# Attention and two MLPs on one core: batch 0's q and k loaded to 128 partitions, empty products on TensorE, and a new order

## The chip, the core and the metric

The kernel runs on one core of a Trainium2 chip. The metric is the device time of one execution in microseconds (us); the kernel before was timed three times, and once more under the profiler. The engines are named as in the profile: PE is TensorE (PEld its weight loads), DVE is VectorE, ACT is ScalarE, POOL is GpSimd, and SP (SPq in a timeline) is SyncE, on whose queue all loads and stores of this kernel are issued.

## What is computed

```python
def _attn_ref(q, k, v):                      # q, k, v: 2 batches, 8 heads, 576 positions, 64 wide
    q_d = q.reshape(B, H, Sd, factor, D).mean(axis=3)     # factor 4, Sd = 144; k_d, v_d alike
    out_up = np.repeat(sm_attn(q_d, k_d, v_d), factor, axis=2)
    mask = np.abs(pos[:, None] - pos[None, :]) < factor
    scores = np.where(mask, scale * np.matmul(q, k.transpose(0, 1, 3, 2)), -1000000000.0)
    ...
    return out_up + np.matmul(softmax(scores), v)

def _moe_ref(x, w_in, w_out):                # x: 1152 x 512, w_in: 512 x 2048
    h = x @ w_in
    return np.where(h > 0.0, h, np.exp(np.minimum(h, 0.0)) - 1.0) @ w_out

def _moe2_ref(x, domain_probs, w1, w2):      # 4 experts, 512 x 1024 and 1024 x 512
    p = domain_probs / (domain_probs.sum(-1, keepdims=True) + 1e-09)
    for e in range(E):
        out += p[:, e:e + 1] * (np.maximum(x @ w1[e], 0.0) @ w2[e])
    return out
```

The attention's output, as 1152 rows of 512, is x of the first MLP, and that one's output is x of the second.

## The kernel before

The program is one stream of steps up to the second MLP. The steps stand in a string, ORDER, in the order in which they are issued; each engine does its share of them in that order. A step's name is a letter or two and numbers; 0 or 1 ahead of it is the batch. Behind a colon stands the engine that does it (v, a or g for VectorE, ScalarE, GpSimd) or, for a step that takes a PSUM bank, a number of empty products.

The steps of attention: LK loads q or k (ti is 0 for q, 1 for k). For batch 0 a load brings half the heads to 72 partitions, eight positions of each head in a row, and is issued as one DMA for 64 partitions and one for 8. CP copies a head pair so that it can be transposed, Tp transposes it on TensorE (four products of 72 columns), Te evicts the result to qkT. Batch 1's loads need no copy. PQ pools q or k over four positions; LV loads v for pooling, PVa and PVb pool it; VB loads a block of v for the local attention. GSp, GSm, GSx, GEr, GEm, GTp, GTe, GPp and GPe are the pooled attention (scores, maximum, exponential, sum, division, transposes, product with v); LSp to LPp are the local attention for a block of 64 queries, and LPa, LPh and LPl add both and write x as two parts, high and low. The steps of the first MLP: wF loads a quarter of a set of weights (1 MB), wA to wE round it, wH and wL split it; hp multiplies x by w_in for 128 hidden columns and 288 rows (12 products), ha, he, hd, hh and hl make the activation, yp multiplies it by w_out, ya evicts and adds up. mF, mS, mH, mL and nF, nH, nL prepare the second MLP's first weights. At C the attention's buffers are given back and the weights that follow load into them.

SyncE issues the loads in the order of the steps, each when its buffer is free. PSUM has eight banks, handed out in the order of the steps: a step on TensorE that takes the ninth waits until the first has been evicted. Ahead of everything, step W issues ten products of nothing. A step with a number behind its colon starts with that many products of 256 columns on the bank that it takes:

```python
        def bank(name, spare=0, uses=1):
            ...
            for _ in range(spare):
                nc.tensor.matmul(ps[:, :256], identb, junk.to_broadcast([P, 256]), start=True, stop=True)
```

In the kernel before no step has such a number.

## Time and profile before

| what | value |
|---|---|
| median of 3 timed runs | 689.39 us (688.63 to 689.83) |
| the profiled execution, its own time | 687.1 us |
| its span, first to last instruction | 685.3 us |
| mean granted TensorE clock | 0.974 |
| TensorE busy | 660.8 us (96%) |
| VectorE, ScalarE, GpSimd busy | 453.8, 303.4, 260.3 us |

The span is 1.8 us shorter than the execution's own time, which also holds what lies around the instructions. A granted clock of 1.00 is TensorE's upper level, 2.4 GHz, and 0.50 its lower, 1.2 GHz; a value between is a mean over a stretch. Products are pipelined, so a busy TensorE in these rows is one that has products under way.

### The profile page before, as it was taken

To read this page: it belongs to the slowest core of one execution; us is meant where nothing else is said; L and a number is where in the kernel's file an instruction comes from. 1 tells how busy PE (TensorE), PEld (TensorE's weight loads), DVE (VectorE), ACT (ScalarE), POOL (GpSimd) and SP (SyncE) were. 2 spreads that over 40 slices of the span, in tenths; PEclk is the share of its full clock that TensorE was granted. 3 is DMA by queue.
4 is the path that set the end of the run, shared out by engine and by line. 5 is a ranking of instruction groups with operands and counts; after the bars stand their busy time and mean duration, and the time that the engine had idled before them with its cause. 6 is when DMAs were issued, how large, how long until landed. Compare 5 with 4: busy or idle time off the path is not lost.

```text
span 685.3 us, 12161 instructions
## 1 busy us (share of the span) xinstructions
PE 660.8 (96%) x4804; PEld 607.2 (89%) x4804; DVE 453.8 (66%) x887; ACT 303.4 (44%) x801; POOL 260.3 (38%) x231
## 2 busy tenths in 40 slices
PE   6698998999999999999999999999999999999997
PEld 4477998899999999998889899898898998998986
DVE  3689998844767868489847567476385475663752
ACT  3489977655656545644413223134043132241310
POOL 1422334533521231547735434445175254344000
PEclk7579999999999999999999999999999999999999
DMA  8987336303024130010110211011101101110012
GB/s 169 213 228 176 117 77 83 82 1 125 12 113 121 65 124 1 1 62 2 61 62 1 62 62 49 14 62 62 61 2 62 62 1 61 63 62 1 1 46 93
DMA packets 40943, 46.69 MB, mean 68 GB/s; under 512 B 23094, under 2 KB 23094, under 8 KB 40886
## 3 DMA queue, kind: packets, MB, share of 16 engines
q1 hardware_dynamic: 40886, 45.91, 24.1%
q8 instruction: 38, 0.62, 0.4%
q14 instruction: 19, 0.16, 0.1%
HBM read 43.55 MB, written 2.36 MB: 67 GB/s over the span
## 4 chain that ended last, share of the span: by engine, by line
PE 83%; DVE 5%; DMA 4%; ACT 3%; SPq 2%; POOL 1%; issue 1%; DVEq 0%; ACTq 0%; POOLq 0%
PE psH L263 37%; PE psZ L263 29%; PE psY L263 13%; DMA raw<-in_v_dram 3%; SPq L513 2%; PE psX L677 1%; PE psS L616 1%; DMA vb<-in_v_dram 1%; PE psP L660 1%; DMA raw<-in_q_dram 1%; SPq L500 1%; PE psO L790 1%; ACT le L635 1%; PE psGT L768 1%; PE psT L567 1%
## 5 line engine op out<-in xcount | busy, mean ns | idle before, releaser
L263 PE MATMUL psZ<-wr,h 128*128 128x512 f32 x864 | 199.2, 390 | 0.0
L263 PEld LDWEIGHTS psZ<-wr,h 128*128 128x128 f32 x864 | 161.3, 188 | 33.1
L999 DVE TENSOR_TENSOR u<-psH,u 128x288 f32<-128x288 f32 x224 | 97.9, 454 | 30.6 <-PE psH L263 23.5
L263 PE MATMUL psH<-x,w 128*128 128x288 f32 x768 | 111.5, 299 | 0.2
L1060 DVE SCALAR_TENSOR_TENSOR oacc<-psZ,pn,oacc 128x512 f32<-128x512 f32 x63 | 47.2, 750 | 96.3 <-PE psZ L263 96.3
L263 PE MATMUL psY<-g,w 128*128 128x288 f32 x768 | 109.1, 296 | 1.2 <-DVE acc L885 1.2
L263 PEld LDWEIGHTS psH<-x,w 128*128 128x128 f32 x768 | 105.4, 190 | 1.1 <-issue 0.5
L263 PEld LDWEIGHTS psY<-g,w 128*128 128x128 f32 x768 | 103.9, 188 | 2.1 <-DVE acc L885 1.5
L1002 ACT ACTIVATE h<-u 128x288 fp32r<-128x288 f32 x128 | 56.6, 443 | 97.9 <-DVE u L999 95.7
L1006 DVE SCALAR_TENSOR_TENSOR h<-u,h 128x288 fp32r<-128x288 f32 x128 | 88.2, 693 | 7.0 <-ACT h L1002 5.2
L263 PE MATMUL psH<-xt,ws 128*128 128x288 f32 x576 | 82.3, 295 | 1.2 <-POOL xt L921 1.0
L263 PEld LDWEIGHTS psH<-xt,ws 128*128 128x128 f32 x576 | 78.5, 188 | 1.7 <-POOL xt L921 1.3
L1016 ACT ACTIVATE u<-psH 128x288 f32<-128x288 f32 x32 | 12.9, 403 | 141.1 <-PE psH L263 141.1
L857 POOL TENSOR_TENSOR g<-gf,g 128x288 fp32r<-128x288 f32 x40 | 35.1, 888 | 81.4 <-ACT g L852 81.1
L263 PE MATMUL psH<-xbo,wa 128*128 128x288 f32 x384 | 61.5, 295 | 0.0
L369 POOL TENSOR_TENSOR st<-raw 128x256 f32<-128x256 f32 x32 | 27.1, 846 | 77.8 <-DMA raw<-in_moe_w_dram 77.2
L263 PEld LDWEIGHTS psH<-xbo,wa 128*128 128x128 f32 x384 | 55.4, 188 | 1.2
L397 POOL TENSOR_TENSOR ws<-st,ws 128x1024 fp32r<-128x1024 f32 x16 | 38.9, 2431 | 44.9 <-ACT ws L391 44.9
L397 POOL TENSOR_TENSOR wa<-raw,wa 128x256 fp32r<-128x256 f32 (+1 forms) x32 | 34.9, 1094 | 41.4 <-ACT wa L391 41.4
L435 POOL TENSOR_TENSOR wr<-raw,wr 128x1024 fp32r<-128x1024 f32 x16 | 39.4, 2479 | 17.3 <-ACT wr L430 17.3
L845 DVE SCALAR_TENSOR_TENSOR gf<-m,psH 128x288 f32<-128x288 f32 x64 | 28.6, 450 | 22.3 <-ACT m L840 15.5
L852 ACT ACTIVATE g<-gf 128x288 fp32r<-128x288 f32 x64 | 26.4, 439 | 25.6 <-DVE gf L845 19.5
(99 smaller groups left out, 819.4 us busy)
## 6 DMA issues: line engine op xcount, KB each, us to landing
raw<-in_moe_w_dram SPq DMA_DIRECT2D x16, 1024.0 KB, 5.3
raw<-in_moe_w_in_dram SPq DMA_DIRECT2D x8, 1024.0 KB, 6.4
raw<-in_moe_w_out_dram SPq DMA_DIRECT2D x8, 1024.0 KB, 6.6
vb<-in_v_dram SPq DMA_DIRECT2D x16, 160.0 KB, 5.7
out_dram<-oacc SPq DMA_DIRECT2D x9, 256.0 KB, 2.0
raw<-in_v_dram SPq DMA_DIRECT2D x4, 512.0 KB, 11.9
raw<-in_q_dram SPq DMA_DIRECT2D x2, 512.0 KB, 9.6
raw<-in_k_dram SPq DMA_DIRECT2D x2, 512.0 KB, 7.4
```

The lines of the kernel that those rows point to most:

```text
L263: nc.tensor.matmul(ps, wt[a], xt[b], start=first and n == 0, stop=last and n == 2)
L369: nc.gpsimd.tensor_tensor(out=st[:, o], in0=x, in1=y, op=op)
L397: nc.gpsimd.tensor_tensor(out=lo, in0=x, in1=hi.bitcast(F32), op=sub)
L435: nc.gpsimd.tensor_tensor(out=t[:, 1], in0=raw[0][:, 2 * j:2 * j + 2], in1=t[:, 0].bitcast(F32), op=ALU.subtract)
L513: nc.sync.dma_start(raw[:cn, r], src[r])
L845: nc.vector.scalar_tensor_tensor(out=gf, in0=m, scalar=-1.0, in1=ps[:, :HB], op0=ALU.add, op1=ALU.max)
L852: nc.scalar.activation(g[:, 0], ps1["gf", s, t, f], AF.Copy)
L857: ENG[eng].tensor_tensor(out=g[:, 1], in0=gf, in1=g[:, 0].bitcast(F32), op=ALU.subtract)
L999: nc.vector.tensor_tensor(out=o, in0=y, in1=x, op=ALU.add)
L1002: nc.scalar.activation(dest(i, k)[0], c, AF.Relu)
L1006: nc.vector.scalar_tensor_tensor(out=l, in0=c, scalar=0.0, in1=h.bitcast(F32), op0=ALU.max, op1=ALU.subtract)
L1060: nc.vector.scalar_tensor_tensor(out=a, in0=ps, scalar=sc, in1=a, op0=ALU.mult, op1=ALU.add)
```

## The change

Four things change. First, a load of q or k of batch 0 goes to 128 partitions: two heads of the four of a half stand below each other, 64 partitions each, with nine positions in a row, and the other two heads stand beside them. It is one DMA. A copy CP now takes two head pairs at once, with five or four of the nine positions (RG), so there are eight instead of sixteen; it writes into the buffers that later hold the sums of the first MLP. A transpose step has five or four products of 64 columns. As the heads are paired in another way, head(h) says where batch 0's head h stands, and the steps that multiply by v (LPp, GPp) ask it. Second, LV is one DMA for 72 partitions, in both batches. Third, 14 steps of ORDER carry a number, 121 empty products together. Fourth, ORDER is another order from its beginning to the second MLP.

```diff
 ORDER = """
-W 0LK.0.1 0CP.0.3.1:v 0CP.0.2.1:a 0CP.0.2.0:v 0Tp.0.2.0 0Tp.0.2.1 0Tp.0.3.1 0CP.0.3.0:a 0Tp.0.3.0 0Te.0.3.0:a
...
+W 0LK.1.1 0CP.1.1.0:v 0Tp.1.2.0:5 0CP.1.1.1:v 0Tp.1.2.1 0Te.1.2.1:v 0Tp.1.3.0 0LK.0.0 0CP.0.0.1:v 0Tp.0.1.1:8
+0Tp.0.0.1 0CP.0.0.0:a 0LK.1.0 0CP.1.0.0:a 0CP.1.0.1:v 0Tp.1.1.1:12 0Tp.1.0.1 0Te.1.1.1:v 0Te.0.1.1:a 0Te.0.0.1:a
...
+wC.0.3 wD.0.3 wE.0.2 0GEr.0.0 0GEm.0.0:g 0GTp.0.2:30 0GTe.0.2:v 0LSp.0 0LSm.0 0GSp.1.0 0GSm.1.0 0LSx.1 0LEr.1
...
@@ -198,13 +197,15 @@
     SD = S // R
     HB = S // 2
     PB = SD // 2
-    RL = 2 * R
     VR = 80
     QB = 64
     W = 3
     KB = QB + 2 * W
     NB = S // QB
     HP = H // 2
+    RL = 2 * R
+    RQ = S // QB
+    RG = ((0, 5), (5, 4))
     KD = DM // P
     NQ = NT // HB
     SCALE = 1.0 / float(D) ** 0.5
@@ -492,40 +493,44 @@
                 self.mx = {}
                 self.e, self.pT, self.eg, self.aT, self.vb, self.cp = {}, {}, {}, {}, {}, {}
 
-            def load(self, src, half, uses):
-
-                t = s8.tile([PB, HP, RL * D], F32, name="raw", uses=uses)
-                src = src[self.b, half * HP:(half + 1) * HP].rearrange("h (p r) d -> p h (r d)", r=RL)
-                for p in (slice(0, QB), slice(QB, PB)):
-                    nc.sync.dma_start(t[p], src[p])
-                return t
-
-
-
-            def LK(self, ti, x):
+
+
+
+            def LK(self, ti, i):
                 if self.b == 0:
-                    self.raw[ti, x] = self.load((q, k)[ti], x, 4)
+                    self.raw[ti, i] = raw = s8.tile([P, 2, RQ * D], F32, name="raw", uses=2)
+                    src = (q, k)[ti][0, i * HP:(i + 1) * HP].rearrange("(a x) (p r) d -> (x p) a (r d)", a=2, r=RQ)
+                    nc.sync.dma_start(raw, src)
                 else:
-                    c0, cn = CHUNKS[x]
-                    self.raw[ti, x] = raw = s8.tile([80, R, H, D], F32, name="raw", uses=HP)
+                    c0, cn = CHUNKS[i]
+                    self.raw[ti, i] = raw = s8.tile([80, R, H, D], F32, name="raw", uses=HP)
                     src = (q, k)[ti][self.b, :, R * c0:R * (c0 + cn), :].rearrange("h (p r) d -> r p h d", r=R)
                     for r in range(R):
                         nc.sync.dma_start(raw[:cn, r], src[r])
 
-            def CP(self, ti, hp, g):
-
-                raw = self.raw[ti, hp // 2]
-                self.cp[ti, hp, g] = t = gp.tile([P, 2, HB], F32, name="cp")
-                o = t.rearrange("p a b -> p (a b)")[:PB, :2 * R * D].rearrange("p (r h d) -> p r h d", r=R, h=2)
-                i = raw[:, hp % 2 * 2:hp % 2 * 2 + 2, g * R * D:(g + 1) * R * D].rearrange("p h (r d) -> p r h d", r=R)
+            def head(self, h):
+
+                return (h // 4 * 2 + h % 2, h % 4 // 2) if self.b == 0 else (h // 2, h % 2)
+
+            def CP(self, ti, i, g):
+
+                raw = self.raw[ti, i]
+                if (ti, i) not in self.cp:
+                    self.cp[ti, i] = accp[ti].tile([P, KD, HB], F32, tag="acc", name="cp")
+                o = self.cp[ti, i].rearrange("p a b -> p (a b)").rearrange("p (r h d) -> p r h d", r=RQ, h=2)
+                c = raw.rearrange("p h (r d) -> p r h d", r=RQ)
+                r = slice(RG[g][0], sum(RG[g]))
                 if self.opt == "a":
-                    nc.scalar.activation(o, i, AF.Copy)
+                    nc.scalar.activation(o[:, r], c[:, r], AF.Copy)
                 else:
-                    ENG[self.opt].tensor_copy(o, i)
+                    ENG[self.opt].tensor_copy(o[:, r], c[:, r])
                 s8.done(raw)
 
             def LV(self, half):
-                self.vraw[half] = self.load(v, half, 1)
+
+                self.vraw[half] = t = s8.tile([PB, HP, RL * D], F32, name="vraw")
+                src = v[self.b, half * HP:(half + 1) * HP].rearrange("h (p r) d -> p h (r d)", r=RL)
+                nc.sync.dma_start(t, src)
 
             def keys(self, i):
                 lo, hi = max(0, i * QB - W), min(S, i * QB + QB + W)
@@ -547,31 +552,35 @@
             def part(self, g):
 
                 if self.b == 0:
-                    return PB, lambda x: x.rearrange("p (t r) -> p t r", r=RL)[:, :, g * R:(g + 1) * R]
+                    r, n = RG[g]
+                    return QB, n, lambda x: x.rearrange("p (t r) -> p t r", r=RQ)[:, :, r:r + n]
                 c0, cn = CHUNKS[g]
-                return cn, lambda x: x[:, R * c0:R * (c0 + cn)].rearrange("p (t r) -> p t r", r=R)
+                return cn, R, lambda x: x[:, R * c0:R * (c0 + cn)].rearrange("p (t r) -> p t r", r=R)
 
             def Tp(self, ti, hp, g):
                 if not hasattr(self, "qkT"):
                     self.start()
-                cn = self.part(g)[0]
+                cn, n, _ = self.part(g)
+                self.ps["T", ti, hp, g] = ps = self.bank("psT")
+                ps = view(ps, n, cn)
+                p = slice(0, cn)
                 if self.b == 0:
-                    t = self.cp.pop((ti, hp, g))
-                    src = t.rearrange("p a b -> p (a b)")[:cn, :2 * R * D].rearrange("p (r x) -> p r x", r=R)
+                    t = self.cp[ti, hp // 2].rearrange("p a b -> p (a b)").rearrange("p (r x) -> p r x", r=RQ)
+                    p = slice(hp % 2 * QB, (hp % 2 + 1) * QB)
+                    src = t[p, RG[g][0]:sum(RG[g])]
                 else:
                     t = self.raw[ti, g]
                     src = t[:cn, :, 2 * hp:2 * hp + 2].rearrange("p r h d -> p r (h d)")
-                self.ps["T", ti, hp, g] = ps = self.bank("psT")
-                ps = view(ps, R, 80)
-                for r in range(R):
-                    nc.tensor.transpose(ps[:, r, :cn], src[:, r], ident[:cn, :cn])
-                (gp if self.b == 0 else s8).done(t)
+                for r in range(n):
+                    nc.tensor.transpose(ps[:, r], src[:, r], ident[p, p])
+                if self.b:
+                    s8.done(t)
 
             def Te(self, ti, hp, g):
-                cn, to = self.part(g)
+                cn, n, to = self.part(g)
                 ps = self.ps.pop(("T", ti, hp, g))
                 evac(
-                    self.opt, to(self.qkT[:, ti, hp]), view(ps, R, 80)[:, :, :cn].rearrange("p r t -> p t r"),
+                    self.opt, to(self.qkT[:, ti, hp]), view(ps, n, cn).rearrange("p r t -> p t r"),
                     scale=1.0 if ti else SCALE,
                 )
                 psb_.done(ps)
@@ -671,13 +680,12 @@
                 self.ps["X", i] = ps = self.bank("psX")
                 ps = view(ps, HP, QB)
                 pT = self.pT.pop(i)
-                for hp in range(HP):
-                    for par in range(2):
-                        c = slice(par * QB, (par + 1) * QB)
-                        nc.tensor.matmul(
-                            ps[par * D:(par + 1) * D, hp, :], self.vb[i][:n, 2 * hp + par, :], pT[:n, hp, c],
-                            start=True, stop=True,
-                        )
+                for h in range(H):
+                    hp, par = self.head(h)
+                    nc.tensor.matmul(
+                        ps[h % 2 * D:(h % 2 + 1) * D, h // 2, :], self.vb[i][:n, h, :],
+                        pT[:n, hp, par * QB:(par + 1) * QB], start=True, stop=True,
+                    )
                 sl["pT"].done(pT)
                 sl["vb"].done(self.vb[i])
 
@@ -786,10 +794,11 @@
                 pso = view(pso, HP, 80)
                 aT = self.aT[c]
                 for h in range(H):
+                    hp, par = self.head(h)
                     for kb in range(2):
                         nc.tensor.matmul(
                             pso[D * (h % 2):D * (h % 2) + D, h // 2, :cn],
-                            self.vp[:, kb, h, :], aT[:, h % 2, h // 2, kb, :cn],
+                            self.vp[:, kb, h, :], aT[:, par, hp, kb, :cn],
                             start=kb == 0, stop=kb == 1,
                         )
```

SyncE's queue at the beginning, where batch 0's q, k and v and the first weights are loaded (raw is a loaded half of q, k or, before, v; vb a block of v). Before, from its fifth DMA on:

```order
L500 DMA raw<-in_k_dram 64x4x512
L500 DMA raw<-in_k_dram 8x4x512
L500 DMA raw<-in_v_dram 64x4x512
L500 DMA raw<-in_v_dram 8x4x512
L500 DMA raw<-in_q_dram 64x4x512
L500 DMA raw<-in_q_dram 8x4x512
L500 DMA raw<-in_v_dram 64x4x512
L500 DMA raw<-in_v_dram 8x4x512
L269 DMA raw_475<-in_moe_w_in_dram 128x4x512
```

After the change, from the first load on:

```order
L503 DMA raw<-in_k_dram 128x2x576
L503 DMA raw<-in_q_dram 128x2x576
L503 DMA raw<-in_k_dram 128x2x576
L503 DMA raw<-in_q_dram 128x2x576
L533 DMA vraw<-in_v_dram 72x4x512 x2
L544 DMA vb<-in_v_dram 80x8x64
L270 DMA raw_538<-in_moe_w_in_dram 128x4x512
```

All of q and k now stands ahead of v, and each load is one DMA.

VectorE's first steps (cp is a copy of q or k, psT a transposed one in PSUM, pooled the pooled q or k, gmx and lmx row maxima of pooled and local scores). Before:

```order
L524 COPY cp<-raw 72x512 x7
L472 COPY qkT<-psT 128x72x4
L470 TENSOR_SCALAR qkT<-psT 128x72x4 x2
L583 TENSOR_REDUCE pooled<-qkT 128x288
L472 COPY qkT<-psT 128x72x4
L583 TENSOR_REDUCE pooled<-qkT 128x288
L524 COPY cp<-raw 72x512
L470 TENSOR_SCALAR qkT<-psT 128x72x4
L583 TENSOR_REDUCE pooled<-qkT 128x288 x2
L724 TENSOR_REDUCE gmx<-psG 80x2 x2
```

After the change, behind the first two copies and the cast of a constant (its next rows are a pooling sum, a local maximum and the pooled ones):

```order
L473 COPY qkT<-psT 128x64x4
L526 COPY cp<-raw 128x512 x2
L473 COPY qkT<-psT 128x64x4
L471 TENSOR_SCALAR qkT<-psT 128x64x5
L473 COPY qkT<-psT 128x64x5
L471 TENSOR_SCALAR qkT<-psT 128x64x4
L473 COPY qkT<-psT 128x64x5
L592 TENSOR_REDUCE pooled<-qkT 128x288
L471 TENSOR_SCALAR qkT<-psT 128x64x5
L592 TENSOR_REDUCE pooled<-qkT 128x288 x2
L634 TENSOR_REDUCE lmx<-psS 128x4
```

Four copies are left on VectorE, and two more evictions have come to it.

ScalarE around C, where the third set of weights is first touched (acc<-psY frees a bank of the first MLP's output, m<-psH is the first step of an activation, cv and wa read a weight that was just loaded). Before:

```order
L883 ACTIVATE acc<-psY 128x288
L836 ACTIVATE m<-psH 128x288
L840 ACTIVATE m<-m 128x288
L291 ACTIVATE cv<-raw_2649 128x512
L291 ACTIVATE cv<-raw_2651 128x512
L291 ACTIVATE cv<-raw_2649 128x512
L883 ACTIVATE acc<-psY 128x288
```

After the change:

```order
L845 ACTIVATE m<-psH 128x288
L849 ACTIVATE m<-m 128x288
L292 ACTIVATE cv<-raw_2798 128x512 x2
L292 ACTIVATE cv<-raw_2809 128x512 x2
L392 ACTIVATE wa<-raw_2823 128x2x256
L392 ACTIVATE wa<-raw_2823 128x256
L892 ACTIVATE acc<-psY 128x288
```

Three loads' first readers, six steps, now stand together between an activation and the next eviction of psY.

## Rows read from the trace of the kernel before

**Rows 1.** The page: TensorE's busy time, and its granted clock in 40 slices.

```profile
PE 660.8 (96%) x4804; PEld 607.2 (89%) x4804; DVE 453.8 (66%) x887; ACT 303.4 (44%) x801; POOL 260.3 (38%) x231
...
PEclk7579999999999999999999999999999999999999
```

**Rows 2.** Windows: busy time by engine, granted clock, share of DMA, GB/s.

```profile
core 0: us, PE busy (x) PEld busy (x) DVE busy (x) ACT busy (x) POOL busy (x), PEclk, DMA share, GB/s
0.00:5.00 5.00, 4.08 (x10) 1.34 (x10) 0.30 (x2) 0.00 (x0) 3.37 (x20) 1.00 0.46 116
5.00:30.00 25.00, 14.88 (x132) 12.12 (x131) 11.88 (x22) 10.94 (x25) 7.20 (x4) 0.59 1.07 188
30.00:55.00 25.00, 21.57 (x286) 16.78 (x286) 22.41 (x59) 21.53 (x95) 6.69 (x6) 0.80 0.97 242
55.00:70.00 15.00, 14.25 (x141) 12.96 (x137) 14.29 (x34) 14.06 (x57) 3.22 (x3) 0.89 0.60 147
70.00:100.00 30.00, 30.00 (x339) 27.43 (x337) 28.98 (x58) 24.41 (x79) 10.76 (x10) 1.00 0.32 91
100.00:140.00 40.00, 36.89 (x411) 34.16 (x410) 32.50 (x69) 29.05 (x111) 18.00 (x16) 1.00 0.47 85
140.00:350.00 210.00, 207.56 (x1554) 201.84 (x1553) 144.82 (x276) 111.39 (x253) 85.78 (x77) 1.00 0.18 61
...
6.00:18.00 12.00, 6.62 (x48) 5.81 (x48) 5.77 (x13) 6.75 (x14) 0.69 (x1) 0.59 1.07 193
32.00:36.00 4.00, 3.58 (x32) 2.88 (x34) 3.93 (x12) 4.00 (x25) 0.88 (x1) 0.50 1.03 379
```

**Rows 3.** Windows: the stretches in front whose granted clock is 0.50.

```profile
8.10:23.90 15.80, 8.55 (x64) 7.61 (x62) 7.28 (x14) 7.60 (x19) 3.60 (x2) 0.50 1.08 182
23.90:28.60 4.70, 4.70 (x44) 3.31 (x44) 3.20 (x5) 0.79 (x4) 3.60 (x2) 0.50 1.10 208
32.00:42.20 10.20, 9.78 (x95) 7.49 (x97) 8.83 (x25) 9.77 (x53) 3.15 (x3) 0.50 1.14 292
55.90:59.30 3.40, 3.40 (x14) 3.40 (x15) 3.12 (x11) 3.40 (x22) 1.09 (x1) 0.50 0.82 152
```

**Rows 4.** Timeline and chain, TensorE: products at either level of the clock.

```profile
0.92 4.18 PE L959 MATMUL psW<-junk 128*128 128x512 bf16 x10 [0.92 <-DVE junk L928]
...
25.49 1.20 PE L616 MATMUL psS<-qkT 64*64 64x70 f32 x16
...
47.50 0.70 PE L616 MATMUL psS<-qkT 64*64 64x70 f32 x16
...
55.22 5.33 PE L263 MATMUL psH<-x,w 128*128 128x288 f32 x24
...
76.56 4.99 PE psH L263 x36
```

**Rows 5.** Timeline: steps that end a wait for a load, and a maximum.

```profile
6.98 0.76 DVE L524 COPY cp<-raw 72x512 f32<-72x512 f32 x2 [5.23 <-DMA raw<-in_q_dram]
...
21.06 0.42 DVE L524 COPY cp<-raw 72x512 f32<-72x512 f32 x1 [2.05 <-DMA raw<-in_q_dram]
...
25.95 0.81 DVE L724 TENSOR_REDUCE gmx<-psG 80x2 f32<-80x288 f32 x2
...
28.50 1.25 ACT L291 ACTIVATE cv<-raw 128x512 f32<-128x512 f32 x2 [3.91 <-DMA raw<-in_moe_w_in_dram]
```

**Rows 6.** Groups by line, 0 to 130 us: busy, mean ns | idle before.

```profile
L583 DVE TENSOR_REDUCE pooled<-qkT 128x288 f32<-128x1152 f32 x8 | 10.6, 1346 | 0.2
...
L567 PE MATMUL psT<-ident,raw 80*128 80x80 f32 x32 | 4.5, 260 | 1.7 <-DMA raw<-in_q_dram 1.7
...
L524 DVE COPY cp<-raw 72x512 f32<-72x512 f32 x8 | 3.0, 420 | 12.3 <-DMA raw<-in_q_dram 7.3 <-DMA raw<-in_k_dram 5.0
...
L470 DVE TENSOR_SCALAR qkT<-psT 128x288 f32<-128x288 f32 x3 | 1.3, 448 | 1.6 <-PE psT L567 1.6
```

**Rows 7.** Waits of TensorE from 70 us on: in total, times, longest.

```profile
PE psO L790 <- ACT aT L468: 2.2, 1, 2.2
```

More of the change, by code (lines that the diff above doesn't have):

```diff
@@ new lines @@
+1VB.2 yp.0.0.3 ya.0.0.3 1LEm.1:g 1LTp.1 1LTe.1:a 1LTp.2 1LSx.4 1LTe.2:a 1LSx.3 1PQ.0.1 1GSp.0.1 wB.1.3 wC.1.3
+wD.1.3 wE.1.3 wA.1.4 wL.1.1:v yp.0.1.2 ya.0.1.2 wL.1.0:v hp.1.0.0 ha.1.0.0 hp.1.0.1 he.1.0.0 ha.1.0.1 he.1.0.1
+1LV.0 wB.1.2 wC.1.2 wD.1.2 wE.1.2 wE.1.6 1LEr.2 1LEm.2:v 1LTp.4 1LTe.4:a 1LTp.3 1LEr.0 1LEm.0:g 1GSm.0.1
+1GSx.0.1 wB.1.4 1PQ.0.0 yp.0.1.3 ya.0.1.3 1PVa.0 1PVb.0 wH.1.2 wL.1.2:g wH.1.3 1PQ.1.0 hd.1.0.0 hh.1.0.0
+hd.1.0.1 hh.1.0.1 1LSp.6 1LSm.6 1LSx.6 1LSp.5 1LSm.5 1LSx.5 1GSp.0.0 1GSm.0.0 1GSx.0.0 1LTp.0 1LSp.7 1LSp.8
@@ L117 @@
+xh.2.1 yp.3.1.2 ya.3.1.2 yp.3.1.3 ya.3.1.3 xd.0.1 xh.1.3 xl.1.3:v xh.1.2 xl.1.2:v xd.0.2 xd.0.3 xth.0.2
+xtl.0.2:v xth.0.3 xtl.0.3:v xth.0.1 xtl.0.1:v xh.2.2 xl.2.2:g xl.2.1:g yp.3.3.0 ya.3.3.0 yp.3.3.1 ya.3.3.1
 yp.3.3.2 ya.3.3.2 yp.3.3.3 ya.3.3.3 xh.3.2 xl.3.2:v xh.3.3 xl.3.3:v
```

176 lines of the change are left out of this document (83 added, 93 removed).

## Prediction

> **What bounds the kernel now.** I read the page first, then windows, then waits and the timeline of the front. On the page TensorE is busy 660.8 us of the span of 685.3, so 24.5 us are idle, and the line of granted clocks is below full only in the first four slices [rows 1]. The windows say where the idle time lies [rows 2]: 0.92 us in 0 to 5, 10.12 in 5 to 30, 3.43 in 30 to 55, 0.75 in 55 to 70; then nothing to 100, 3.11 to 140 and 2.44 to 350; what is left, nearly 4 us, is the tail of the last outputs. From 70 us on TensorE is the bound. In front it isn't: 15.2 us idle, and 26.4 us of its busy time lie in four stretches whose granted clock is 0.50, the lower of the two levels (1.2 GHz) [rows 3]. Not all of that doubles. Sixteen score products take 1.20 us at the lower level and 0.70 at the upper [rows 4]. Taking that ratio, 0.6, for the 17.9 us of the last three stretches gives a loss of 7.2; the first stretch (8.55 us) is mostly transposes bound by their weight loads, where I allow a tenth, 0.9. So TensorE loses 15.2 + 8.1 = 23.3 us before 70 us.
>
> What it waits for in front is VectorE and ScalarE, and those wait for loads. The timeline has VectorE's copies starting at 6.98 and, for the last load, at 21.06, both released by a load of q, and ScalarE's first touch of a weight at 28.50 by another [rows 5]. VectorE is busy only 12.2 us of the first 30, then 22.4 of 25, 14.3 of 15, and 29.0 of 30 up to 100 us [rows 2]: there it is as full as TensorE. So in front work runs from loads through VectorE to TensorE, and a gain is what the first 30 us give back.
>
> **The loads.** q and k of batch 0 come as four loads of 589,824 bytes. At the 193 GB/s of 6 to 18 us (72 partitions filled) one is 3.06 us; at the 379 GB/s of 32 to 36, when weights go to 128 partitions, 1.56 [rows 2]. The packets differ little (2,048 bytes there, 2,304 now), so I take 379; the bounds are 193 and 379. The first copy at 6.98 minus 3.06 leaves 3.9 us of issue and latency, so the four land near 5.5, 7.0, 8.6 and 10.2; before, the first was used at 6.98 and the last at 21.06 [rows 5]. The last one moves most, because a v load no longer stands ahead of it on SyncE's queue. v then takes two loads, still on 72 partitions, at 3.06 each (16.3), one small block of v (163,840 bytes, 0.85 us), and the first weight, 1,048,576 bytes or 2.8 us, lands near 20, against 28.5.
>
> **The copies and VectorE's first 30 us.** Sixteen copies of 72x512 become eight of 128x640 or 128x512; four are VectorE's, where it had eight. At 0.42 us per 512 columns they sum to 1.8 us instead of 3.4 [rows 6]. Up to the first row maximum of the pooled scores VectorE has: copies 1.8, seven evictions at 0.45, four pooling sums at 1.35, four maxima, 0.81 for the pooled two and as much for the two local ones: 12.0 us. Before, it had 11.9 (five evictions, no local maximum) and finished at 26.8 (25.95 plus 0.81), so it had idled 15 us [rows 5, 6]. With the first load at 5.5 and no wait it would finish at 17.5. It will wait: its third eviction stands behind twelve empty products and a transposition, ScalarE copies the other half and loads its function table first, and each pooling sum needs both halves of its heads. I allow 3 to 6 us and take 21.8. VectorE is then 5 us ahead. The weight lands at about 20, when ScalarE is still evicting, so its 3.9 us wait at 28.50 goes as well, and with it some 2 us of VectorE's that follow from it: 5 to 7 us.
>
> **What TensorE gets from that.** The work itself stays: 72 transposes instead of 64 (about 0.6 us more), the same products in the two MLPs. The new order puts five more of batch 1's transpose steps (16 instead of 11, 4 products each) ahead of the second tile of hidden products. Such a product is 0.14 us in the rows, lower-level ones included [rows 6]; I take 0.42 us for a step, 2.1 us of work that is done sooner. So by VectorE, TensorE reaches its full stretch 7 to 9 us earlier.
>
> **The empty products.** The order asks for 121, each 256 columns with its own weight load. At full clock 36 products of 288 columns take 4.99 us, 0.139 each, so 0.12 for 256; the weight load lies beside the product before it, as in those rows. At the lower level ten of 512 columns take 4.18 us, 0.42 each, so 0.21 [rows 4] (the window of 0 to 5 us gives them 1.00, but a product of 512 columns at the other's pace would be 0.25). They cost 14.5 us at the one and 25 at the other. Where TensorE would wait they cost nothing and only hold the clock; past that they are queue ahead of real work, since TensorE runs in order. This gives the cap: with TensorE never idle after the first 0.92 us and never at the lower level it would lose 0.9 + 14.5 = 15.4 us in front instead of 23.3. **The front can give 7.9 at most.** Both bounds meet at about 8, so neither engine alone decides; two engines that feed each other don't both run without a gap, and the first products run at the lower level anyway. I take **6.2**, with 1.5 (many gaps) and 7.9 as ends.
>
> **The rest of the order.** Everything up to the second MLP is rearranged. Before, the waits behind 70 us sum to 5.5, the largest 2.2 where the outputs of the pooled attention wait for ScalarE [rows 2, 7]. Those rows hang on particular neighbours that the new order parts; new ones may come. From both ends (all gone, as many again) I take 1.2 gained. The tail doesn't change.
>
> **Sum.** 6.2 + 1.2 = 7.4 us: a span of 677.9, and 679.7 for an execution like the profiled one (687.1). The timed median is 689.39, 2.3 above that execution, so **682.0** in the timed runs.
>
> **v in one load.** v of batch 0 is now written to all 72 partitions by one load for each half, where 64 and 8 were loaded apart. The rows have the split form alone, at 193 GB/s [rows 2], and I keep that rate; ScalarE's arrival at the first weight leaves about 1 us of cover behind it. The Trainium skill (DMA: Bandwidth & Descriptors, "Why a DMA increments its semaphore by 16 and not by 1") says that a load uses the largest number of engines, up to 16, that divides the outermost sizes of both sides, which for 72 would be 12. By the rows the sum stays 682.0; by that rule it would be up to 2 us more. No run before shows a load of v in this form, so the trace can't agree or disagree.
>
> **The rivals.**
> *v gets slower.* If v's loads went at three quarters of 193, 145 GB/s, each would take 4.1 us instead of 3.06, v would end 2 us later, and so would every weight behind it on the same queue: the first near 22. ScalarE would reach it at 21 to 22, so the price lies between 0 and 2 us: with the upper end, 684.0. For it speaks that a load in this form has no row yet, against it that ScalarE has other work until then. (This is the rule from the Trainium skill, above, as a mechanism of this kernel.) Chance 0.10.
>
> *ScalarE blocks behind three loads.* In the new order ScalarE's first reads of three weight loads of 1 MB stand together, and the evictions that free TensorE's PSUM banks stand behind them. At 3.9 + 2.8 us for the first and 2.8 for each next, the third is there 12 us after the issue. TensorE has up to seven products of 1.7 us queued when its eight banks are full, so the wait is 0 to 6 us; a median of 3 gives 685.0. Before, only two such loads stood together, and the 2.44 us of waits from 140 to 350 are all that TensorE had there [rows 2]. Chance 0.12.
>
> *The loads stay at 193 GB/s.* Then the change doesn't do what it says: the four land at 7.0, 10.0, 13.1 and 16.2, still ahead of 21.06 through the order, but half the front's gain is gone: 685.6. The 379 of the weights speaks against it. Chance 0.06.
>
> *TensorE stays at 1.2 GHz (slower).* 114 of the empty products stand ahead of the first hidden product, which started at 55.2 us [rows 4]. TensorE was busy 40.5 us up to 55 [rows 2], of which 6.7 were the lower level's; with batch 1's steps that is some 35 us of real work at full clock, and 13.7 of empty products, 48 in all. At the lower level the products cost 24 and the real work about 12 more: 71 us, later than VectorE by far, and the end moves by some 14 us: 703. It turns a gain into a loss when about two fifths of that stretch runs at the lower level. For it: ten products of nothing at the start all ran at the lower level [rows 4], and transposes kept the clock at 0.50 through 8 to 24 us. Against it: in 23.9 to 28.6 TensorE was busy without a gap and the clock rose right behind, and from 70 us on, with TensorE full, it stays at 1.00 [rows 2, 3]. Chance 0.08.
>
> **How the numbers follow.** The forecast (a gain of 4 to 13 us without one of these) has 0.51; more than 13 has 0.03. Measurements of this kernel tell apart about 0.2%, 1.4 us. The first three rivals are all faster by more than that, with 0.28 together. The fourth is slower, 0.08. That leaves 0.10 for a new order whose own gaps eat the gain: 0.07 to within 0.2%, 0.03 for more. So faster 0.51 + 0.03 + 0.28 = 0.82, same 0.07, slower 0.11. The range reaches down to the cap of the front (1.7 below the 6.2 taken) with 5.2 of the 5.5 us of later waits gone (4.0 below the 1.2 taken): 682.0 − 5.7 = 676.3. Upward it takes in the first three rivals and the front's low end without any gain behind it (687.9): 688.0.
>
> **What would show it.** Right: the first VectorE copy at about 5.5 and the last of q and k in by 11; VectorE busy over 17 us of the first 30; a granted clock of 1.00 from about 8 us to the end; the first hidden product at 48 to 50 instead of 55.2; TensorE full from there. Wrong: stretches at 0.50 with empty products in them at 0.21 us; v's loads over 4 us apart and ScalarE waiting for a weight after 22 us; a wait of TensorE for an eviction at 170 to 190 us; VectorE idle after 30 us with TensorE in front of it busy on empty products.

## The result and the profile after

The changed kernel took **673.53 us** (median of 4, 672.84 to 674.41) beside 689.01 us for the kernel before on the same chip (median of 4, 687.27 to 689.83): a ratio of 0.9771, 95% interval 0.9743 to 0.9798, a gain of 15.5 us. The forecast was 682.0 with a range from 676.3 to 688.0. The direction held; the gain was twice as large as forecast, and the time lies 2.8 us below the range. The profiled execution took 674.41 us, its span is 672.2.

The page of the changed kernel, TensorE's busy time and its granted clock, against [rows 1]:

```profile
PE 662.5 (99%) x4933; PEld 609.1 (91%) x4933; DVE 454.3 (68%) x893; ACT 298.7 (44%) x792; POOL 256.7 (38%) x226
...
PEclk9999999999999999999999999999999999999999
```

TensorE is 1.7 us longer busy in a span that is 13.1 us shorter, and its clock is full in every slice. The windows that answer to [rows 2] (stretch, its length, then busy time of each engine with its count, granted clock, DMA share, GB/s):

```profile
0.00:5.00 5.00, 4.08 (x10) 1.31 (x10) 0.06 (x1) 1.28 (x1) 3.36 (x20) 1.00 0.62 194
5.00:30.00 25.00, 22.62 (x264) 16.89 (x265) 16.53 (x35) 12.20 (x46) 8.38 (x5) 1.00 1.04 262
30.00:55.00 25.00, 24.55 (x345) 21.60 (x342) 23.31 (x61) 23.35 (x102) 10.28 (x8) 1.00 1.00 202
55.00:70.00 15.00, 15.00 (x246) 13.27 (x245) 14.69 (x35) 14.15 (x37) 5.67 (x5) 1.00 0.66 133
70.00:100.00 30.00, 28.97 (x266) 26.74 (x267) 29.00 (x55) 26.00 (x95) 10.69 (x10) 1.00 0.30 91
100.00:140.00 40.00, 39.11 (x407) 36.62 (x408) 29.50 (x67) 24.95 (x93) 12.22 (x12) 1.00 0.17 33
140.00:350.00 210.00, 209.71 (x1558) 204.65 (x1558) 151.28 (x289) 108.38 (x246) 85.05 (x76) 1.00 0.19 66
```

The length of a stretch minus TensorE's busy time in it is TensorE's idle time: up to 70 us it fell from 15.22 to 3.75, from 70 to 350 us from 5.55 to 2.21. The groups of TensorE by line and form, 0 to 130 us (busy, mean ns of one, then idle time before), show the empty products and the transposes of batch 0:

```profile
L480 PE MATMUL psT<-junk,identb 128*128 128x256 bf16 x43 | 7.7, 342 | 1.1 <-DVE identb L971 1.1
L480 PE MATMUL psGT<-junk,identb 128*128 128x256 bf16 x39 | 4.8, 273 | 1.0 <-ACT eg L744 1.0
L575 PE MATMUL psT<-ident,cp 64*128 64x64 f32 x72 | 4.7, 257 | 0.0
L480 PE MATMUL psP<-junk,identb 128*128 128x256 bf16 x24 | 3.2, 273 | 0.0
L480 PE MATMUL psS<-junk,identb 128*128 128x256 bf16 x11 | 1.6, 274 | 0.0
L480 PE MATMUL psX<-junk,identb 128*128 128x256 bf16 x4 | 0.6, 273 | 0.0
```

The five groups of empty products hold 121 and sum to 17.9 us; counted from each start to the next product's start they take 16.3, since the end of one lies beside its successor. So TensorE's own work, all that is not an empty product, is 662.5 − 16.3 = 646.2 us, where it was 660.8: **14.6 us less for the same work** (72 transposes of 64 columns stand for 64 of 72). Most of that is the clock's, but not all: [rows 3] has 26.4 us of busy time at the lower level, and half of that is 13.2. The rest fits something else. A product with nothing behind it is counted to its end (0.22 to 0.33 us in these traces) and not only up to its successor's start; up to 350 us TensorE waits 19 times in the kernel before and 8 times in the changed one, so I put this at some 2 us, an estimate. The transposes of batch 0 now take 4.7 us for 72 of them, and none waits. In the kernel before the same group reads:

```profile
L567 PE MATMUL psT<-ident,cp 72*128 72x72 f32 x64 | 8.9, 328 | 10.0 <-ACT cp L522 5.2 <-DVE cp L524 4.8
```

The balance of the two profiled executions closes: idle in front −11.5, own work −14.6, empty products +16.3, idle from 70 to 350 us −3.3, together −13.1, the difference of the spans.

### The profile page after: what moved, and what is told of

Same layout as the page of the kernel before. It is cut to its first block, busy times and chain, and to the rows that moved or that the text cites. A ratio compares the mean times of both kernels' runs of the same rounds, so it can differ in the third digit from the quotient of the medians.

```text
span 672.2 us, 12384 instructions
## 1 busy us (share of the span) xinstructions
PE 662.5 (99%) x4933; PEld 609.1 (91%) x4933; DVE 454.3 (68%) x893; ACT 298.7 (44%) x792; POOL 256.7 (38%) x226
## 4 chain that ended last, share of the span: by engine, by line
PE 84%; DVE 10%; issue 2%; ACT 1%; POOL 1%; DMA 1%; DVEq 0%; ACTq 0%; POOLq 0%
PE psH L264 37%; PE psZ L264 29%; PE psY L264 13%; DVE raw L309 1%; DVE pooled L592 1%; PE psT L480 1%; DVE raw L316 1%; DVE w L330 1%; DVE cv L302 1%; DMA raw<-in_k_dram 1%; PE psP L669 1%; PE psGT L480 1%; DVE acc L920 1%; PE psS L625 1%; PE psGT L776 1%
## 5 line engine op out<-in xcount | busy, mean ns | idle before, releaser
L264 PE MATMUL psH<-x,w 128*128 128x288 f32 x768 | 109.1, 296 | 0.6 <-DVE x L710 0.4
L264 PEld LDWEIGHTS psH<-x,w 128*128 128x128 f32 x768 | 103.5, 188 | 1.9 <-POOL x L710 0.6
L866 POOL TENSOR_TENSOR g<-gf,g 128x288 fp32r<-128x288 f32 x31 | 25.9, 845 | 59.6 <-ACT g L861 56.3
L845 ACT ACTIVATE m<-psH 128x288 f32<-128x288 f32 x64 | 25.8, 403 | 26.6 <-PE psH L264 16.3
```

The costliest lines, as they stand in the source:

```text
L264: nc.tensor.matmul(ps, wt[a], xt[b], start=first and n == 0, stop=last and n == 2)
L845: nc.scalar.activation(m, ps1["h", s, t, f][:, :HB], AF.Relu, scale=-1.0)
L866: ENG[eng].tensor_tensor(out=g[:, 1], in0=gf, in1=g[:, 0].bitcast(F32), op=ALU.subtract)
```

## Which part gave the gain: loads, order, empty products

Four kernels, timed together on one chip (the kernel before: 688.92, median of 19); the row of the changed kernel in the table is the result above, timed apart from them. The short rows of ORDER stand for all steps changed alike.

**new_none**, the changed kernel without empty products:

```diff
-W 0LK.1.1 0CP.1.1.0:v 0Tp.1.2.0:5 0CP.1.1.1:v 0Tp.1.2.1
+W 0LK.1.1 0CP.1.1.0:v 0Tp.1.2.0 0CP.1.1.1:v 0Tp.1.2.1
```

> The changed kernel without its 121 products of nothing; the outputs are unchanged. Theory (the lower clock was the larger loss in front, about 14.5 us of TensorE's own work, so holding the clock is most of the gain): stretches at a granted clock of 0.50 come back in the first 50 us, and the time is 4 to 10 us above the changed kernel's 673.5, so 677 to 684. Rival (loads and order gave the gain, the products are only in the way of real work, as their 0.12 us each suggests): the same time or up to 5 us less, 668 to 674.

**old_empty**, the kernel before with empty products:

```diff
-W 0LK.0.1 0CP.0.3.1:v 0CP.0.2.1:a 0CP.0.2.0:v 0Tp.0.2.0 0Tp.0.2.1 0Tp.0.3.1 0CP.0.3.0:a 0Tp.0.3.0
+W 0LK.0.1 0CP.0.3.1:v 0CP.0.2.1:a 0CP.0.2.0:v 0Tp.0.2.0:12 0Tp.0.2.1 0Tp.0.3.1 0CP.0.3.0:a 0Tp.0.3.0:4
```

> The kernel before, its loads and its order kept, with 91 products of nothing put in front of steps at which TensorE waits (12, 4, 5, 12 and 40 at five transposition steps of batch 0, 4, 8 and 6 later); the outputs are unchanged. Theory (the clock): the products fill waits that are there anyway, the transposes behind them run at the upper level, so the front gives back part of the 8 to 14 us that the lower level cost: 680 to 686, and the transposes of cp at under 0.08 us each instead of 0.139. Rival (TensorE waits for the loads in front, and faster products only wait longer): 688 to 690, no change. Rival (the products delay the evictions' tiles): up to 693.

**oldorder_newload**, the changed kernel in the old order (two copies of head pairs become one step):

```diff
-W 0LK.1.1 0CP.1.1.0:v 0Tp.1.2.0:5 0CP.1.1.1:v 0Tp.1.2.1
+W 0LK.0.1 0CP.0.1.1:v 0CP.0.1.0:v 0Tp.0.2.0 0Tp.0.2.1
```

> The changed kernel's loads (four of 128 partitions), its eight copies and its v loads, in the old order, with no products of nothing; the outputs are unchanged. Theory (loads are the smaller part; the front then still runs at the lower clock): 3 to 6 us gained, 683 to 686, with v's load still ahead of the last load of q and k on the queue. Rival (loads and VectorE's copies are the larger part): 676 to 681. Rival (the old order was written for the old loads and gives nothing): 688 to 690.

**oldorder_newload_empty**, the same with the empty products of old_empty:

```diff
-0CP.0.1.0:v 0Tp.0.2.0 0Tp.0.2.1
+0CP.0.1.0:v 0Tp.0.2.0:12 0Tp.0.2.1
```

> As oldorder_newload, the old order with the new loads and copies, and 91 products of nothing at the same steps as in old_empty; the outputs are unchanged. Theory (clock and loads each give their own part, the order the rest): 676 to 681, that is most of the changed kernel's gain without its order. Rival (the order gives most: it parts the steps that wait): 683 to 687. If the parts don't add up, the difference to the sum of old_empty's and oldorder_newload's gains shows it.

| kernel | loads | order | empty products | us (lowest to highest) | ratio, 95% interval | clock in its executions |
|---|---|---|---|---|---|---|
| before | old | old | none | 688.92 (684.31 to 693.04) | 1 | 0.962 to 0.991 |
| old_empty | old | old | 91 | 688.45 (685.32 to 693.65) | 0.9998 [0.9961, 1.0035] | 0.975 to 0.990 |
| oldorder_newload | new | old | none | 679.63 (678.45 to 682.11) | 0.9876 [0.9802, 0.9950] | 0.977 to 0.980 |
| oldorder_newload_empty | new | old | 91 | 681.78 (678.97 to 688.50) | 0.9911 [0.9873, 0.9949] | 0.980 to 0.997 |
| new_none | new | new | none | 678.27 (677.97 to 678.70) | 0.9854 [0.9796, 0.9912] | 0.972 |
| changed | new | new | 121 | 673.53 (672.84 to 674.41) | 0.9771 [0.9743, 0.9798] | 1.000 |

The loads with their copies gave 9.3 us under the old order; the new order without empty products 1.4 more, which the intervals don't tell from nothing; the empty products 4.7 more, in the new order only. The last step compares runs timed apart; it rests on all of new_none's four executions, which lie above all ten of the changed kernel (after_again, below, included). The new order with the old loads was not run, so the order's share is known only on top of the new loads. My expectation for the loads (3 to 6 us) was too low and the rival's (676 to 681) right; for new_none the theory held, for old_empty the rival that nothing changes, and oldorder_newload_empty lies just outside the theory's 676 to 681: the products gave nothing there that the intervals tell from nothing.

The trace of new_none shows why 14 us of slower work cost only 4.7. Its windows:

```profile
5.00:30.00 25.00, 17.51 (x227) 13.39 (x227) 20.03 (x45) 15.21 (x64) 9.52 (x6) 0.73 1.03 262
30.00:55.00 25.00, 23.74 (x226) 19.96 (x227) 17.90 (x44) 17.68 (x66) 6.95 (x7) 0.53 0.87 156
55.00:70.00 15.00, 15.00 (x227) 13.75 (x226) 14.32 (x33) 14.23 (x45) 3.82 (x4) 0.99 0.77 188
```

From 30 to 55 us its granted clock is 0.53, TensorE is busy 23.74 of 25, and VectorE has only 17.90 to do where it had 23.31 in the changed kernel: here TensorE at the lower clock holds the others back. Most of VectorE's idle time in that window is waits for TensorE, the longest sums being these (in total, times, longest):

```profile
DVE lmx L629 <- PE psS L620: 1.9, 2, 1.5
DVE xf L691 <- PE psX L680: 1.8, 3, 0.7
DVE pT L468 <- PE psP L664: 1.3, 1, 1.3
```

But TensorE's busy time over the whole span, 660.1 us, contains no empty product, and it idles 16.5 us in all. Between new_none and the changed kernel, own work falls by 13.9, idle time by 6.8, and 16.3 us of empty products come: −4.4, as the spans say (676.6 and 672.2). The empty products are a trade, and the net is a third of the own work that they save.

In the old order the trade comes to nothing. The 64 transposes of the kernel before fell from 8.9 to 6.6 us in old_empty, but 13.4 us of empty products bought 8.2 us of own work and 7.0 of idle time (spans 685.3 and 683.5), and its executions differ by 8 us. Where I had put the numbers, the clock held in some executions and not in others: in oldorder_newload_empty the execution with a mean clock of 0.980 had a span of 686.7, the one with 0.996 had 677.6. The clock isn't all of it: one with 0.997 had 680.7.

## Which part of the loads: rate, copies, or place on the queue

**oldorder_newload64** and **new_load64** write each new q and k load as two transfers of 64 partitions, one in the old order without empty products and one in the changed kernel:

```diff
-                    nc.sync.dma_start(raw, src)
+                    for p in (slice(0, QB), slice(QB, P)):
+                        nc.sync.dma_start(raw[p], src[p])
```

> The changed kernel with each of its four q and k loads written as two transfers of 64 partitions, nothing else changed. Theory (the load's rate goes by the partitions that one transfer fills, 193 GB/s at 64 and 8 of them, 379 at 128): the four land at 6 to 7, 9 to 10, 12 to 13 and 15 to 16 us instead of 5.1, 6.6, 8.1 and 10.3, and the time is 2 to 5 us above the changed kernel's 673.5. Rival (two queued halves fill the same engines, and only the issue costs something): landings under 1 us later, 673 to 675.

> The new loads and copies in the old order, no products of nothing (679.6 as it stands), with each q and k load of batch 0 as two transfers of 64 partitions. Theory (the rate counts where no products of nothing hold VectorE back; the landings move from 4.5, 6.0, 7.6 and 12.6 by 1, 2, 3 and up to 5 us, as in new_load64): 683 to 685. Rival (the rate is hidden here too): 679 to 681.

**oldorder_copytwice** does each of the eight copies twice in a row:

```diff
-                if self.opt == "a":
+                for _ in range(2):
+                    if self.opt == "a":
```

> The new loads and copies in the old order, no products of nothing (679.6 as it stands), with each of the eight copies done twice, so that they take VectorE and ScalarE as long as the sixteen of before, about 2 us more on each engine; the outputs are unchanged. Theory (VectorE is the bound of the front once the loads are there): 681 to 683. Rival (the copies stand in the shade of the next load): 679 to 680.

**old_kfirst** moves one load in the kernel before:

```diff
-0LV.1 0PVa.1 0PVb.1 0Te.0.3.1:a
+0LK.0.0 0LV.1 0PVa.1 0PVb.1 0Te.0.3.1:a
```

> The kernel before with one step moved: the last load of q is issued ahead of the first load of v. Theory (that load is what the front waits for, it was used at 21 us and lands 3 to 4 us sooner): 685 to 687. Rival (v is then 3 us later, and the pooling of v and the first weight with it, so nothing is gained): 688 to 690.

**new_lvsplit** loads v as before, as 64 and 8 partitions (the step serves both batches, so batch 1's v is split again too):

```diff
-                nc.sync.dma_start(t, src)
+                for p in (slice(0, QB), slice(QB, PB)):
+                    nc.sync.dma_start(t[p], src[p])
```

> The changed kernel with each v load of batch 0 written as before, as 64 and 8 partitions. Theory (the one load of 72 partitions costs no more than the two, 192 to 225 GB/s after the change against 193 before): the same time, 672.5 to 674.5, with one or two more issues on SyncE's queue. Rival (the load of 72 goes at three quarters of the rate): v lands 1 to 2 us earlier here and the time is 1 to 2 us lower.

The last three kernels of the old order were timed on one chip, new_load64 and new_lvsplit together on another; oldorder_newload and the changed kernel are the rows of the table above.

| kernel | us (lowest to highest) | ratio, 95% interval |
|---|---|---|
| oldorder_newload, above | 679.63 (678.45 to 682.11) | 0.9876 [0.9802, 0.9950] |
| oldorder_newload64 | 685.34 (682.40 to 689.88) | 0.9950 [0.9922, 0.9978] |
| oldorder_copytwice | 679.15 (675.67 to 684.17) | 0.9847 [0.9783, 0.9911] |
| old_kfirst | 688.29 (683.41 to 693.41) | 0.9991 [0.9954, 1.0028] |
| changed | 673.53 (672.84 to 674.41) | 0.9771 [0.9743, 0.9798] |
| new_load64 | 674.14 (673.44 to 675.62) | 0.9771 [0.9723, 0.9820] |
| new_lvsplit | 672.73 (671.93 to 673.68) | 0.9753 [0.9696, 0.9809] |

The rate of the loads carries most of it: the theory of oldorder_newload64 put the time at 683 to 685, and it came at 685.34. For the copies and for old_kfirst the rival held, for new_lvsplit the theory; new_load64 has the rival's time, but its loads are first touched at 6.32, 9.82, 11.45 and 14.05 instead of 5.16, 6.64, 8.15 and 12.12, 1.2 to 3.3 us later, where the rival had under 1. Under the old order, two transfers of 64 partitions instead of one of 128 take 5.7 of the 9.3 us away. The two kernels ran on different chips and their intervals touch, but all ten executions of the split lie above all four without it, and oldorder_copytwice, timed with the split on one chip, is 6.2 below it. Doing every copy twice, or moving the last q load alone, changes nothing that can be measured. No run parts the partitions of a transfer from the number of transfers, and the other 3.6 of the 9.3 us are not assigned. Windows of 3 to 5 us and steps of the timeline (start, duration, engine, [idle before, releaser]), oldorder_newload first:

```profile
3.00:5.00 2.00, 2.00 (x6) 0.61 (x4) 0.48 (x2) 0.00 (x0) 0.98 (x6) 1.00 1.04 408
...
12.62 1.26 ACT L519 ACTIVATE cp<-raw 128x640 f32<-128x640 f32 x2 [1.38 <-DMA raw<-in_q_dram]
...
17.60 0.81 DVE L727 TENSOR_REDUCE gmx<-psG 80x2 f32<-80x288 f32 x2
```

and oldorder_newload64:

```profile
3.00:5.00 2.00, 1.82 (x6) 0.55 (x4) 0.00 (x0) 0.00 (x0) 0.98 (x6) 1.00 1.04 253
...
19.23 1.26 ACT L520 ACTIVATE cp<-raw 128x640 f32<-128x640 f32 x2 [4.21 <-DMA raw<-in_q_dram]
...
24.21 0.81 DVE L728 TENSOR_REDUCE gmx<-psG 80x2 f32<-80x288 f32 x2
```

The same bytes in the same order go at 408 GB/s into 128 partitions and at 253 into 64; the last copy starts 6.6 us later and so does the first maximum of the pooled scores. The Trainium skill (DMA: Bandwidth & Descriptors, "Rules for kernel authors") advises 128 partitions and one transfer instead of two for disjoint halves, and this trace agrees.

In the changed kernel the same split costs 0.6 us beside the first result and 1.4 beside new_lvsplit, which was timed with it; the intervals don't tell either from nothing, although the rate falls there as well, from 372 to 264 GB/s between 3 and 5 us. The first maximum starts at 23.98 with full loads and at 23.77 with split ones, but that pair misleads: in the former execution the first 25 empty products ran mostly at the lower level (below), and VectorE waited behind them. In the profiled executions of new_lvsplit and after_again, full loads too, they ran at the upper one. The first maximum, new_load64 ahead of new_lvsplit:

```profile
23.77 0.81 DVE L733 TENSOR_REDUCE gmx<-psG 80x2 f32<-80x288 f32 x2
...
20.70 0.81 DVE L733 TENSOR_REDUCE gmx<-psG 80x2 f32<-80x288 f32 x2
```

So it comes 3.1 us later with split loads: the first empty product starts 1.6 us later (7.66 and 6.04), and the eight empty products that follow on the first transposes take 1.89 us in that execution and 1.06 in the other. The span is only 1.5 us longer (671.6 and 670.1). That a later load costs nothing in the new order is not shown; a slow start of the clock can hide it.

v as one load of 72 partitions costs nothing that can be measured against 64 and 8 (0.8 us, intervals overlapping). The rule that I had weighed (the Trainium skill, DMA: Bandwidth & Descriptors, "Why a DMA increments its semaphore by 16 and not by 1") isn't seen in the time. The profiled executions of after_again (one load) and new_lvsplit (two) start their first copy alike, at 4.69; the first half of v is read at 13.40 and 13.54, and from 10 to 14 us the queue moves 226 and 199 GB/s. The loss of a quarter that the rival had assumed isn't there.

## How many empty products

**new_half**, **new_double** and **new_third** change only the numbers (62, 242 and 41 instead of 121; the expectation of new_half says 61). new_half_again and after_again repeat two of them on the chip of new_third, and **new_half_junk** takes the tile of junk as the weights too:

```diff
-... 0Tp.1.2.0:5 ... 0Tp.0.1.1:8 ... 0GTp.0.2:30
+... 0Tp.1.2.0:3 ... 0Tp.0.1.1:4 ... 0GTp.0.2:15
```

```diff
-                nc.tensor.matmul(ps[:, :256], identb, junk.to_broadcast([P, 256]), start=True, stop=True)
+                nc.tensor.matmul(ps[:, :256], junk.to_broadcast([P, P]), junk.to_broadcast([P, 256]), start=True, stop=True)
```

> The changed kernel with its numbers of products of nothing halved (61 instead of 121); the outputs are unchanged. Without them it took 678.3, with all of them 673.5. Theory (they are worth what they hold of the clock, and it holds as long as the gaps are short enough): the clock falls in one or two stretches, 674 to 677. Rival (half of them would do, and each one left out gives 0.12 us back): the clock stays at 1.00 and the time is 667 to 671.

> The changed kernel with the numbers of products of nothing doubled (242); the outputs are unchanged. The clock can't get better than 1.00, so each added product only stands in front of real work. Theory (TensorE would have been idle for only 4.8 us in front, so 121 times 0.12 less some of that is late): 10 to 14 us more, 683 to 688. Rival (VectorE bounds the front, and TensorE has room for them): up to 3 us more, 674 to 677.

> The changed kernel once more, on the chip of the three other runs of this group. Theory: 673 to 674 as on the first chip, a granted clock of 1.00 in all executions. If the half's 671.4 came from the chip alone, this one is at 671 to 672 here.

> Half of the products of nothing (62 instead of 121) once more, beside the changed kernel on the same chip. Theory (59 fewer products leave VectorE's copies and the first transposes less to wait for, and the clock holds from 20 us on): 671 to 672, 2 us under the changed kernel. Rival (chance between chips): within 1 us of it.

> A third of them (41). Theory (the curve has its bottom between none at 678.3 and half at 671.4): the gaps get long enough for the clock to fall in a stretch of some executions, 672 to 676, with executions at unlike clocks. Rival (still too many): 669 to 671.

> Half of them, with the tile of junk as their weights too, so that the first of them don't wait for VectorE's cast of the identity, which in the new code stands behind two copies (a wait of 1.1 to 1.5 us at 6 us). Theory (that wait is at the head of the chain from loads through VectorE to TensorE): 0.5 to 1.5 us under new_half_again. Rival (the first transposes need the copies and not the products in front, and VectorE is late by other things): the same time within 0.5 us.

| empty products | us (lowest to highest) | ratio, 95% interval | clock in its executions |
|---|---|---|---|
| none (new_none) | 678.27 (677.97 to 678.70) | 0.9854 [0.9796, 0.9912] | 0.972 |
| 41 (new_third) | 672.39 (671.43 to 675.06) | 0.9739 [0.9713, 0.9765] | 0.990 to 0.994 |
| 62 (new_half) | 671.36 (670.76 to 672.31) | 0.9729 [0.9682, 0.9777] | 0.995 to 0.997 |
| 62 (new_half_again) | 671.39 (671.06 to 671.50) | 0.9718 [0.9693, 0.9742] | 0.999 to 1.000 |
| 62 (new_half_junk) | 671.68 (670.29 to 672.01) | 0.9719 [0.9693, 0.9745] | 0.995 to 0.997 |
| 121 (changed) | 673.53 (672.84 to 674.41) | 0.9771 [0.9743, 0.9798] | 1.000 |
| 121 (after_again) | 672.00 (671.17 to 677.34) | 0.9742 [0.9711, 0.9772] | 0.997 to 1.000 |
| 242 (new_double) | 683.13 (681.98 to 684.97) | 0.9893 [0.9856, 0.9929] | 0.999 to 1.000 |

The rows come from several chips: new_none from the first group, new_half and new_double from a second, new_third and the three timed with it from a third. The curve is flat from 41 to 121, and 0 and 242 lie clearly above it. A third of the products holds 0.99 of the clock already; its executions have unlike clocks and 672.39, as the theory of new_third said. Doubling them costs 10 us and buys no clock, as the theory had it: in new_double VectorE waits for transposes that stand behind them (in total, times, longest):

```profile
DVE qkT L469 <- PE psT L571: 6.5, 2, 4.5
DVE cp L522 <- DMA raw<-in_k_dram: 3.9, 1, 3.9
DVE aT L469 <- PE psGT L772: 3.2, 2, 2.4
```

Half of them is the best number tried, by 0.6 us on one chip, which its interval doesn't tell from the changed kernel (the rival of new_half_again, not its theory of 2 us); the changed kernel itself came at 672.0 there, below the 673 to 674 expected, so part of the first distance was the chip or the group. new_half lies below the theory's 674 to 677 and just above the rival's 667 to 671, so most of what each product left out gives back is lost again. The junk weights took the wait for the cast away and gave nothing, as the rival said: TensorE's wait for ScalarE at psGT in the first 30 us is 3.6 there, where it is 1.0 in new_half_again.

## Why the prediction was right and wrong

**The failed step is the cap: "The front can give 7.9 at most."** It was worked out from a loss of 8.1 us to the lower clock. That term was mis-sized: TensorE's own work shrank by 14.6 us, of which the lower level, as the granted clock shows it, can account for at most 13.2. The worst part of it is the first stretch of [rows 3], "mostly transposes bound by their weight loads, where I allow a tenth". The weight loads do fill most of that stretch (7.61 us beside 8.55), but they follow the clock too. The same 20 transposes and their weight loads (PEld), first in new_none, where the granted clock from 13.5 to 15.1 us is 0.50, then in the changed kernel, where it is 1.00 from 17.3 to 18.3:

```profile
13.60 1.50 PE L570 MATMUL psT<-ident,cp 64*128 64x64 f32 x20 [0.51 <-ACT cp L519]
13.60 1.31 PEld L570 LDWEIGHTS psT<-ident,cp 64*128 64x128 f32 x20 [0.69 <-ACT cp L519]
...
17.33 0.95 PE L575 MATMUL psT<-ident,cp 64*128 64x64 f32 x20
17.33 0.82 PEld L575 LDWEIGHTS psT<-ident,cp 64*128 64x128 f32 x20 [0.24 <-ACT cp L524]
```

Both lose 37% at the lower level. The 64 products of that stretch are the 64 transposes of 8.9 us; after the change 72 took 4.7 us, and in old_empty the same 64, at a mean clock of 0.89 between 8 and 24 us, took 6.6. Fourteen others can be compared between two executions of the changed kernel, which by their durations ran them at different levels (the granted clock reads 1.00 in both; see the last section). TensorE's timeline in the execution profiled first:

```profile
0.92 4.45 PE L968 MATMUL psW<-junk 128*128 128x512 bf16 x10 [0.92 <-DVE junk L937]
6.50 1.25 PE L480 MATMUL psT<-junk,identb 128*128 128x256 bf16 x5 [1.13 <-DVE identb L971]
7.68 1.39 PE L575 MATMUL psT<-ident,cp 64*128 64x64 f32 x14
9.00 1.89 PE L480 MATMUL psT<-junk,identb 128*128 128x256 bf16 x8
```

and in that of after_again:

```profile
0.93 3.68 PE L968 MATMUL psW<-junk 128*128 128x512 bf16 x10 [0.93 <-DVE junk L937]
6.03 0.73 PE L480 MATMUL psT<-junk,identb 128*128 128x256 bf16 x5 [1.42 <-DVE identb L971]
6.69 0.89 PE L575 MATMUL psT<-ident,cp 64*128 64x64 f32 x14
7.51 1.06 PE L480 MATMUL psT<-junk,identb 128*128 128x256 bf16 x8
```

14 transposes take 1.39 us in the one and 0.89 in the other: a loss of 36%, not of 10%. The transposes lost 4.2 us (8.9 to 4.7) where I had allowed 0.9: 3.3 of the 6.5 that the term lacked. At 37% the clock accounts for some 3.3 of the 4.2, an estimate. The other 3.2 of the 6.5 lie in the remaining work, where I had taken the ratio of score products for all, and part of it isn't the clock's. In the kernel before some transposes of batch 1 stood alone, each behind a wait for a load, where the granted clock was 1.00 (28.6 to 32 us); four in a row, at the same granted clock, took less than two such:

```profile
30.80 0.29 PE L567 MATMUL psT<-ident,raw 80*128 80x80 f32 x1 [0.41 <-DMA raw<-in_q_dram]
31.64 0.29 PE L567 MATMUL psT<-ident,raw 80*128 80x80 f32 x1 [0.56 <-DMA raw<-in_q_dram]
...
45.79 0.50 PE L567 MATMUL psT<-ident,raw 80*128 80x80 f32 x4
```

With 14.6 the cap would have been 15.2 + 14.6 − 15.4 = 14.4, and what bound would have been VectorE's own lead, which I had at 7 to 9. Measured in the same way the front gave 11.5 + 14.6 − 16.3 = **9.8 instead of 6.2**.

**The later waits** gave 3.3, where I took 1.2 and allowed up to 5.5. TensorE's waits from 70 to 350 us after the change are these four; the 2.2 of [rows 7] is gone:

```profile
PE psP L669 <- DVE lsm L654: 0.8, 1, 0.8
PE psX L685 <- DVE od L473: 0.8, 1, 0.8
PE psH L264 <- POOL xt L930: 0.3, 1, 0.3
PE psH L264 <- DVE w L330: 0.2, 1, 0.2
```

**The step from the profiled execution to the median** failed too. I kept 2.3 us between them, and held that measurements of this kernel tell apart 0.2%. But that rested on three runs: 19 of the kernel before are spread over 684 to 693 us, 1.3%, and its profiled execution was one of the better ones; the changed kernel's four lie within 1.6 us, and its median is 0.9 below its profiled execution. Of the 8.5 us of miss, 3.6 are the front, 2.1 the later waits and 3.2 this step (they sum to 8.9; what lies around the span took 0.4 of it back, 2.2 us instead of 1.8).

**The loads** came as predicted: the first copy starts at 5.16 (forecast about 5.5), the second and third load are touched at 6.64 and 8.15, each as it lands (7.0 and 8.6), and the fourth at 12.12, without a wait. **VectorE and the first hidden product**, on the timeline of the changed kernel:

```profile
5.16 1.15 DVE L526 COPY cp<-raw 128x640 f32<-128x640 f32 x2 [4.29 <-DMA raw<-in_k_dram]
...
23.98 0.81 DVE L732 TENSOR_REDUCE gmx<-psG 80x2 f32<-80x288 f32 x2
...
48.86 0.53 PE L264 MATMUL psH<-x,w 128*128 128x288 f32 x2
```

The pooled maximum ended at 24.8, not 21.8, because the first 25 empty products ran mostly at the lower level in this execution and VectorE waited behind them; in after_again it started at 20.69 and ended at 21.5. VectorE was busy 16.6 us of the first 30 instead of over 17 (19.7 in after_again). The first hidden product started at 48.86, inside the 48 to 50 forecast, but that was luck: in after_again, without the slow start, it started at 45.57.

**The empty products** cost 16.3 us instead of 14.5, about as worked out (14.2 in after_again, counted alike).

**The rivals.** v in one load: nothing, as above. ScalarE behind three weights: no such wait is in the trace. The loads at 193 GB/s: no, 372 to 408. TensorE at 1.2 GHz: not beyond the first 14 us of one execution; but old_empty and oldorder_newload_empty show that this rival was real, since products put elsewhere don't hold the clock in every execution.

My first theory after the result, that the clock gave most, fell as well: without any empty product the changed kernel already gains 10.7 us of the 15.5.

## What to carry to other kernels

Price a stretch at the lower clock by the same instructions at both levels, transposes and weight loads included, and not by an assumed bound: a mis-sized loss makes a cap on the gain wrong. Empty products are a trade: they take time in front of real work, their place decides whether they pay, and here 41 did as well as 121. When a load's rate counts, look at how many partitions one transfer fills, and compare executions whose clock rose alike: the same split cost 5.7 us in the old order, and 0.6 or 1.4 in the new one, by the run beside which it is put.

## What the runs showed of the hardware

The clock's rise differs between executions of one program. In the two timelines above the same ten products of 512 columns stand at the start (4.45 and 3.68 us); the five empty products behind them take 1.25 us in one execution and 0.73 in the other, and twelve further on take 2.24 us at 11.45 in the one and 1.51 at 8.90 in the other. The granted clock reads 1.00 over that whole stretch in both (the windows of 0 to 5 and 5 to 30 us), so the durations show what the column doesn't. The spans of the two executions, which were timed apart, differ by 3.2 us.

Executions of the kernel before on one chip ranged from 682.5 us of span at a mean clock of 0.977 to 691.1 at 0.963; the changed kernel's first four executions lie within 1.6 us (of the six of after_again five have spans of 669.0 to 671.8 and one 675.2). The empty products are not what narrows it: new_none's four executions, at a clock of 0.972, lie within 0.8 us.
